# Moving the maxima products around the value products in a two-layer attention and GLU kernel

## The chip, the cores and the metric

The kernel runs on one core of one Trainium2 chip. The metric is device time in microseconds (us) of one execution; the kernel before was timed three times. Besides these times there is one profiled execution, from whose trace all rows below come.

## The reference

Four residual layers on x (2048 tokens, 448 features, float32): attention, gated unit, attention, gated unit, each on a layer-normalised input and with the same weights in both rounds. Attention has 16 heads of width 28 that share one key and one value head.

```python
q = (x @ wq).reshape(B, S, H, Dh).transpose(0, 2, 1, 3)
k = x @ wk
v = x @ wv
scores = einsum("bhqd,bkd->bhqk", q, k) * (Dh ** -0.5)
p = softmax(scores, axis=-1)
o = einsum("bhqk,bkd->bhqd", p, v)
attn = o.transpose(0, 2, 1, 3).reshape(B, S, H * Dh) @ wo

h = sigmoid(x @ w_gate) * (x @ w_up)
glu = h @ w_down

x = x + attn(layernorm(x)); x = x + glu(layernorm(x))   # twice
```

## The kernel before, in words

Tokens are cut into 16 **units** of 128 queries and keys into 16 **key tiles** of 128, so one attention layer has 16 x 16 = 256 **steps**, one for each unit and key tile; two layers have 512. Numbers that need more than half precision are carried as two float16 parts.

One step needs these products on TensorE (the profile's PE):

- four **scores** products `s` (L566): keys against queries, 96 rows deep, 128 x 512 results, four heads each. ScalarE (ACT) turns each into `P` by an exponential (L570), which frees the PSUM bank of `s`.
- one **values** step `pv` (L580 or L584): P against the values. It consists of four products side by side, each with 32 output columns. Most steps keep P in float32 (L584, two instructions to each product in the trace); at key tiles 0, 4, 8 and 12 of well-filled steps GpSimd (POOL) splits P into two float16 parts first (L603, L604), and L580 multiplies these.
- two halves of **maxima** products `mx` (L509). Softmax subtracts the row maximum, and the kernel finds it one unit ahead: it multiplies once more, 32 rows deep, and VectorE (DVE) reduces each 128 x 512 result to its maximum (L512), which frees its PSUM bank. One call of the generator `mx_gen` gives two such products, which stand in different row groups of the array; `group` calls it twice, which gives four products, one in each row group.
- **filler**: projections and the gated unit of earlier tokens (`gp`, `up`, `qp`, `kv` at L369, `dn` at L789, `wo` at L697), full 128 x 128 products that a `Filler` hands out in slices, so many ns of estimated work to a slice.

All of these but `pv` draw their PSUM results from one pool of seven banks, `psf` (L51, L98, L505 to L506, L565). The eighth bank holds the running sum of `pv`. A new tile takes a bank whose last tile has been read, and where that reading is still under way, the product waits for the engine that reads.

```python
ps = {h: psf.tile([128, 512], F32, tag=BANKS["m"], name="mx", bufs=NBK[BANKS["m"]])
      for h in (hh, hh + 1)}
for h in ps:
    nc.tensor.matmul(ps[h][:, :nk], qh[32 * h:32 * h + 32, g], KK[l][32 * h:32 * h + 32, 1, ks],
                     start=True, stop=True, tile_position=(32 * h, 0))
for h in ps:
    nc.vector.tensor_reduce(mp[:, g, h, kb:kb + 1], ps[h][:, :nk], axis=AX.X, op=OP.max)
```

The order of the work is fixed when the program is built (the kernel schedules by hand): every engine runs its instructions in the order in which the Python code emits them. In the loop over steps (L1174 to L1220) a string of letters sets that order, one pass through the string for two steps. The program calls such a pass an order; the texts below say **pass**.

- `F`: a slice of filler. Before it gives products it also emits what was put off: evaluations of finished filler results on DVE and ACT.
- `S`: one scores product and its exponential, and conversions of P that are due.
- `M`: `group`, four maxima products and their four reductions. `m`: one call of the generator, two products and two reductions.
- `P`: one values step, from a queue of finished steps.
- `T`: `finish`, which transposes the maxima of a finished unit (`mt`, L549, 16 output columns), copies them on DVE (L551) and sends them into the queries' tile `QS`.
- `X`: end of a step: deals with side work (normalisation, output projection of finished units), sets the new filler rate.

```python
order = FULL if rate > LEANR else LEAN
```

`rate` is the filler left per step in ns, and `LEANR` is 600. So passes with much filler use the string `FULL`, and passes with little, at the beginning of either layer, use `LEAN`.

In the built program the maxima products stand in groups of four 396 times and in pairs 220 times before the change; four pairs make one LEAN pass, so there are 55 of these. The scores, values, maxima and filler products are the same in number after the change as before.

Of the kernel before, what the change touches and what calls it, by code (L numbers as in the profile page):

```python
# [19 lines left out]
def interleaved_layers_kernel(ctx: ExitStack, tc: tile.TileContext, x, wq, wk, wv, wo, wg, wu, wd, out, layers=2):  # L20
# [577 lines left out]
    def convert():  # L598
        while conv:
            P, g = conv.pop(0)  # L600
            p, e = P[g], CA[g]
            h = wk1.tile([128, 2, 512], F16, name="PH", bufs=PX)
            {"A": nc.scalar.copy, "V": nc.vector.tensor_copy, "P": nc.gpsimd.tensor_copy}[e](h[:, 0], p)  # L603
            nc.gpsimd.tensor_tensor(h[:, 1], p, h[:, 0], op=OP.subtract)  # L604
            P[g] = h
# [534 lines left out]
    for b, g in sorted(qnew):  # L1140
        fill.add(qrest(b, g), QCH)

    FULL = "FSFSFSFSTPPXMFSFSFSFSFXM"
    LEAN = "FSFSmFSFSPTXmFSFSmFSFSPTXm"
    PLAG = 1
    PARTS = [False]

# [6 lines left out]
    for l in range(layers):  # L1154
# [19 lines left out]
        while step < U * KT:  # L1174
            order = FULL if rate > LEANR else LEAN
            for o in order:
                u, kt = divmod(step, KT)
                if o == "S":
                    su, skt = divmod(sn // 4, KT)
                    if sn < 4 * U * KT:  # L1180
                        scores(l, su, skt, sn % 4, P)
                        convert()
                        if order is FULL and skt in KS and l * U * KT + step >= FROM and (sn % 4 == 0 or PARTS[0]):
                            PARTS[0] = sn % 4 < 3
# [76 lines left out]
```

## Time and profile before

| what | us |
|---|---|
| median of three runs | 2257.43 |
| the three runs | 2257.43, 2257.6, 2254.36 |
| the profiled execution, its own time | 2257.6 |
| span of its trace | 2255.8 |
| PE busy | 2202.9 |
| DVE busy | 1673.9 |
| ACT busy | 1397.3 |
| POOL busy | 1045.8 |

The profiled execution is one of the three runs. Its span goes from the first to the last instruction; 1.8 us lie around it. The granted TensorE clock averages 0.997 of full speed. PE rows are pipelined and their ends are modelled, so the start of one row and the start of the next tell how long a product holds the array; the busy time alone does not.

### The profile page before, as it was taken

What the parts mean: (1) busy time and instruction counts of PE and PEld (TensorE: products, weight loads), DVE (VectorE), ACT (ScalarE), POOL (GpSimd) and SP (SyncE); (2) the same over time, 40 slices, a digit from 0 to 9 for tenths busy, and PEclk for the clock granted to TensorE, in tenths of its full rate; (3) what the DMA queues carried; (4) which work ended last, traced back from release to release, by engine and by line L of the source; (5) the groups of instructions that cost most, each with busy time, mean ns of one, the idle gap of its engine ahead of it and who ended that gap; (6) DMA issues with size and microseconds to landing.
All of it is one profiled execution on the core that took longest, in us unless ns stands there. A gap on an engine that the chain in (4) does not pass through costs nothing. (4 is left out here: it accounts for less than half of the span.)

```text
span 2255.8 us, 43048 instructions
## 1 busy us (share of the span) xinstructions
PE 2202.9 (98%) x16336; PEld 1049.5 (47%) x16336; DVE 1673.9 (74%) x2921; ACT 1397.3 (62%) x2567; POOL 1045.8 (46%) x1363
## 2 busy tenths in 40 slices
PE   8999999999999999999999999999999999999999
PEld 6322244544545444454573224545454544445457
DVE  7898887878778887774458887878787877878322
ACT  4677766666666666666425676666666666666641
POOL 4378451555445554546402014545545455454540
PEclk9999999999999999999999999999999999999999
DMA  6734542323313232332341113223232313232233
GB/s 154 212 105 133 184 158 61 93 77 103 112 52 106 67 90 80 98 96 79 102 145 57 31 47 103 85 85 101 60 94 63 102 59 102 80 95 89 78 99 123
DMA packets 224400, 217.53 MB, mean 96 GB/s; under 512 B 154048, under 2 KB 185536, under 8 KB 224192
## 3 DMA queue, kind: packets, MB, share of 16 engines
q1 hardware_dynamic: 217200, 198.89, 30.0%
q0 software_dynamic: 3680, 12.09, 1.4%
q10 hardware_dynamic: 3312, 3.79, 0.5%
q8 instruction: 128, 2.10, 0.4%
q14 instruction: 80, 0.66, 0.1%
HBM read 175.37 MB, written 23.59 MB: 88 GB/s over the span
## 5 line engine op out<-in xcount | busy, mean ns | idle before, releaser
L570 ACT ACTIVATE P<-s 128x512 f32<-128x512 f32 x2048 | 1141.3, 599 | 565.0 <-PE s L566 544.7
L512 DVE TENSOR_REDUCE mp<-mx 128x1 f32<-128x512 f32 x2048 | 1266.7, 681 | 300.6 <-PE mx L509 295.4
L566 PE MATMUL s<-QS,KK 96*128 96x512 f16 x2048 | 740.3, 381 | 21.8 <-DVE mp L512 9.2
L369 PEld LDWEIGHTS <-wgu 128*128 128x128 f16 x4928 | 459.5, 97 | 254.1 <-issue 91.6
L604 POOL TENSOR_TENSOR PH<-P,PH 128x512 f16<-128x512 f32 x384 | 458.7, 1195 | 30.8
L603 POOL CAST PH<-P 128x512 f16<-128x512 f32 x384 | 248.5, 647 | 471.5 <-ACT P L570 471.5
L584 PE MATMUL pv<-P,VV 128*32 128x512 f32 x3328 | 418.5, 599 | 0.0
L369 PE MATMUL gp<-XT,wgu 128*128 128x256 f16 x2464 | 386.1, 272 | 0.8 <-DVE mp L512 0.7
L369 PE MATMUL up<-XT,wgu 128*128 128x256 f16 x2464 | 385.3, 272 | 1.1 <-ACT P L570 0.4
L789 PE MATMUL dn<-WD,h 128*128 128x448 f16 x1344 | 330.4, 353 | 0.0
L509 PE MATMUL mx<-KK,QH 32*128 32x512 f16 x2048 | 257.2, 384 | 5.1 <-ACT P L570 3.1
L566 PEld LDWEIGHTS <-KK 96*128 96x128 f16 x2048 | 188.4, 97 | 136.0 <-issue 62.3
L509 PEld LDWEIGHTS <-QH 32*128 32x128 f16 x2048 | 62.2, 91 | 344.8 <-issue 343.3
L789 PEld LDWEIGHTS <-h 128*128 128x128 f16 x1344 | 124.7, 98 | 138.6 <-issue 23.7
L584 PEld LDWEIGHTS pv<-P,VV 128*32 128x32 f32 x3328 | 86.4, 109 | 167.5 <-issue 146.3
L764 DVE SCALAR_TENSOR_TENSOR h<-th,h 128x512 f16<-128x512 f32 x112 | 99.5, 888 | 48.4 <-ACT h L763 48.4
L763 ACT ACTIVATE h<-th 128x512 f16<-128x512 f32 x112 | 70.3, 628 | 88.0 <-DVE th L760 86.9
L760 DVE SCALAR_TENSOR_TENSOR th<-th,up 128x512 f32<-128x512 f32 x112 | 76.0, 679 | 57.2 <-PE up L369 51.7
L675 POOL TENSOR_TENSOR lb<-pvs,lb 128x512 f32<-128x512 f32 x32 | 40.7, 1270 | 138.3 <-DMA lb<-sums 119.7
L752 ACT ACTIVATE th<-gp,gsc 128x512 f32<-128x512 f32 x112 | 76.8, 686 | 42.3 <-PE gp L369 41.8
L369 PE MATMUL qp<-XT,WQ 128*128 128x512 f16 x352 | 98.4, 386 | 0.7 <-DVE ktl L412 0.7
L329 POOL TENSOR_SCALAR rs<-mv 128x1 f32<-128x1 f32 x48 | 11.0, 229 | 178.6 <-DVE mv L324 178.6
(164 smaller groups left out, 1102.9 us busy)
## 6 DMA issues: line engine op xcount, KB each, us to landing
wgu<-wgu_d SPq DMA_DIRECT2D x224, 512.0 KB
QS<-qd SPq DMA_DIRECT2D x384, 32.0 KB
lb<-sums SPq DMA_DIRECT2D x120, 64.0 KB
wgu_d<-sgu POOLq DMA_DIRECT2D x14, 512.0 KB, 3.8
qd<-qst POOLq DMA_DIRECT2D x16, 256.0 KB, 2.7
xr<-in_A_x_dram SPq DMA_DIRECT2D x16, 224.0 KB
QH<-qd SPq DMA_DIRECT2D x28, 128.0 KB
x2d<-x SPq DMA_DIRECT2D x16, 224.0 KB
```

The costliest lines, as they stand in the source:

```text
L369: nc.tensor.matmul(ps, a, b, start=n == 0, stop=n == 10)
L509: nc.tensor.matmul(ps[h][:, :nk], qh[32 * h:32 * h + 32, g], KK[l][32 * h:32 * h + 32, 1, ks], start=True, stop=True, tile_position=(32 * ...
L512: nc.vector.tensor_reduce(mp[:, g, h, kb:kb + 1], ps[h][:, :nk], axis=AX.X, op=OP.max)
L566: nc.tensor.matmul(s, KK[l][0:96, 0, kt * 128:(kt + 1) * 128], QS[l, u][:, g].rearrange("p h n -> p (h n)"), start=True, stop=True)
L570: nc.scalar.activation(p, s, AF.Exp, scale=ESC)
L584: nc.tensor.matmul(v[32 * g:32 * g + 32], VV[l][:, kt], P[g], start=kt == 0, stop=kt == KT - 1, tile_position=(0, 32 * g))
L603: {"A": nc.scalar.copy, "V": nc.vector.tensor_copy, "P": nc.gpsimd.tensor_copy}[e](h[:, 0], p)
L604: nc.gpsimd.tensor_tensor(h[:, 1], p, h[:, 0], op=OP.subtract)
L752: defer(lambda: nc.scalar.activation(th, gp.rearrange("p j n -> p (j n)"), AF.Tanh, scale=gsc))
L760: nc.vector.scalar_tensor_tensor(t, th, 1.0, up.rearrange("p j n -> p (j n)"), op0=OP.add, op1=OP.mult)
L764: defer(lambda: nc.vector.scalar_tensor_tensor(h[:, 1], t, 2.0 ** -17, h[:, 0], op0=OP.mult, op1=OP.subtract), 1)
L789: nc.tensor.matmul(p, hs[f // 2][:, a, o:o + 128], WD[:, f, c], start=n == 0, stop=n == 3 * FC - 1)
```

## The change

Two strings change, and nothing else:

```diff
-    FULL = "FSFSFSFSTPPXMFSFSFSFSFXM"
-    LEAN = "FSFSmFSFSPTXmFSFSmFSFSPTXm"
+    FULL = "FSFSFSFSTMPPXMFSFSFSFSFX"
+    LEAN = "FSFSFSFSmPTXmFSFSFSFSmPTXm"
```

In FULL, the `M` that stood at the end of a pass, after the last filler slice, now stands in front of the two values steps `PP`; the other `M` stays behind them. So eight maxima products, which were two groups of four with four scores and filler between them on either side, now stand close together, with only the values steps between, and the eight scores follow each other with filler alone between. In LEAN, the `m` that stood between the second and the third score now stands behind the fourth, in front of `P`.

On PE, a FULL pass in the built program before. The rows are in program order; `[waits X_49]` names the engine whose reading of the bank (or whose data) the row waits for; LDWEIGHTS loads the weights of the product behind it.

```order
L566 MATMUL s<-QS,KK 128x512 [waits DVE_49]
L584 MATMUL pv<-P,VV 32x512 x8
L509 LDWEIGHTS QH
L509 MATMUL mx<-KK,QH 128x512 [waits Activation_49]
L509 LDWEIGHTS QH
L509 MATMUL mx<-KK,QH 128x512 [waits DVE_49]
L509 LDWEIGHTS QH [waits PE_49]
L509 MATMUL mx<-KK,QH 128x512 [waits Activation_49]
L509 LDWEIGHTS QH
L509 MATMUL mx<-KK,QH 128x512 [waits DVE_49]
L369 LDWEIGHTS wgu
L369 MATMUL up<-XT_9966,wgu 128x256
```

The same place on PE after the change:

```order
L566 MATMUL s<-QS,KK 128x512 [waits Activation_49]
L509 LDWEIGHTS QH
L509 MATMUL mx<-KK,QH 128x512 [waits Activation_49]
L509 LDWEIGHTS QH
L509 MATMUL mx<-KK,QH 128x512 [waits Activation_49]
L509 LDWEIGHTS QH
L509 MATMUL mx<-KK,QH 128x512 [waits Activation_49]
L509 LDWEIGHTS QH [waits PE_49]
L509 MATMUL mx<-KK,QH 128x512 [waits Activation_49]
L584 MATMUL pv<-P,VV 32x512 x8
L509 LDWEIGHTS QH
L509 MATMUL mx<-KK,QH 128x512 [waits Activation_49]
```

The group of four now stands right behind the last score, and all four of its products wait for exponentials; a second group follows the values. Over the whole program, 971 maxima products waited for ACT and 1060 for DVE before, 1210 and 824 now; of the scores, 996 waited for ACT and 1032 for DVE before, 788 and 1238 now.

On PE, part of a LEAN step in the second layer before:

```order
L566 MATMUL s<-QS,KK 128x512 [waits DVE_49]
L509 LDWEIGHTS QH
L509 MATMUL mx<-KK,QH 128x512 [waits Activation_49]
L509 LDWEIGHTS QH
L509 MATMUL mx<-KK,QH 128x512 [waits DVE_49]
L566 LDWEIGHTS KK
L566 MATMUL s<-QS,KK 128x512 [waits DVE_49]
L566 LDWEIGHTS KK
L566 MATMUL s<-QS,KK 128x512 [waits Activation_49]
L584 MATMUL pv<-P,VV 32x512 x4
L509 LDWEIGHTS QH
L509 MATMUL mx<-KK,QH 128x512 [waits Activation_49]
```

The same after the change:

```order
L566 MATMUL s<-QS,KK 128x512 [waits Activation_49]
L566 LDWEIGHTS KK
L566 MATMUL s<-QS,KK 128x512 [waits DVE_49]
L509 LDWEIGHTS QH
L509 MATMUL mx<-KK,QH 128x512 [waits DVE_49]
L509 LDWEIGHTS QH
L509 MATMUL mx<-KK,QH 128x512 [waits Activation_49]
L584 MATMUL pv<-P,VV 32x512 x4
L509 LDWEIGHTS QH
L509 MATMUL mx<-KK,QH 128x512 [waits DVE_49]
L509 LDWEIGHTS QH
L509 MATMUL mx<-KK,QH 128x512 [waits Activation_49]
```

The pair that parted the four scores now stands between them and the values.

On DVE, in FULL passes of the first layer before (`th` and `h` are filler work of the gated unit, `rc` a reciprocal):

```order
L512 TENSOR_REDUCE mp<-mx 128x1 x4
L658 RECIPROCAL rc<-rc 128x16
L512 TENSOR_REDUCE mp<-mx 128x1 x4
L760 SCALAR_TENSOR_TENSOR th<-th,up 128x512
L512 TENSOR_REDUCE mp<-mx 128x1 x4
L764 SCALAR_TENSOR_TENSOR h<-th,h 128x512
```

And after, in the same part of the program:

```order
L512 TENSOR_REDUCE mp<-mx 128x1 x8
L658 RECIPROCAL rc<-rc 128x16
L760 SCALAR_TENSOR_TENSOR th<-th,up 128x512
L512 TENSOR_REDUCE mp<-mx 128x1 x8
L764 SCALAR_TENSOR_TENSOR h<-th,h 128x512
```

The reductions of the maxima now stand eight in a row, with the other work of DVE between the eights.

## The prediction

> **What bounds the kernel now.** I read the page's head first, then the busy time by stages, then who waits for whom on PE, then two stretches of the timeline.
>
> ```profile
> span 2255.8 us, 43048 instructions
> PE 2202.9 (98%) x16336; PEld 1049.5 (47%) x16336; DVE 1673.9 (74%) x2921; ACT 1397.3 (62%) x2567; POOL 1045.8 (46%) x1363
> ...
> 100.00:300.00 200.00, 187.17 (x1104) 52.66 (x1105) 173.79 (x314) 150.22 (x290) 120.80 (x106) 0.99 0.48 148
> 300.00:1050.00 750.00, 737.45 (x5639) 357.56 (x5632) 586.94 (x1004) 484.09 (x876) 382.98 (x521) 1.00 0.29 87
> 1200.00:1350.00 150.00, 146.32 (x855) 38.17 (x852) 131.27 (x225) 101.77 (x191) 16.40 (x29) 1.00 0.15 43
> 1350.00:2110.00 760.00, 756.75 (x5807) 366.27 (x5810) 599.83 (x999) 496.97 (x893) 396.26 (x496) 1.00 0.28 83
> ...
> PE s L566 <- DVE mp L512: 9.2, 28, 0.6
> PE s L566 <- ACT P L570: 5.6, 25, 0.3
> PE mx L509 <- ACT P L570: 3.1, 8, 1.1
> ```
>
> The stage rows give, after the stretch and its length, the busy time of PE, PEld, DVE, ACT and POOL. Two stages with few weight loads (100 to 300 and 1200 to 1350 us) run LEAN; the two long ones, 1510 us together, run FULL. PE is busy nearly throughout, and its waits for PSUM banks come to some 18 us in all: PE bounds the kernel. DVE stands at 78 to 79% in the FULL stages (586.94 of 750, 599.83 of 760) and at 87 to 88% in LEAN. So what PE no longer does is gained, as long as banks come free in time; that second condition is where the change can lose.
>
> The timeline of one FULL pass shows both sides. Columns: start, duration, engine, line, operation, tiles, shapes, count.
>
> ```profile
> 601.06 0.38 PE L566 MATMUL s<-QS,KK 96*128 96x512 f16 x1
> ...
> 601.28 0.38 PE L369 MATMUL gp<-XT,wgu 128*128 128x256 f16 x2
> ...
> 602.60 0.60 PE L369 MATMUL up<-XT,wgu 128*128 128x256 f16 x4
> ...
> 603.13 0.40 PE L509 MATMUL mx<-KK,QH 32*128 32x512 f16 x4
> ...
> 603.46 0.72 PE L369 MATMUL up<-XT,wgu 128*128 128x256 f16 x5
> 603.55 2.48 DVE L512 TENSOR_REDUCE mp<-mx 128x1 f32<-128x512 f32 x4 [0.36 <-PE mx L509]
> ...
> 605.98 0.38 PE L566 MATMUL s<-QS,KK 96*128 96x512 f16 x1
> ...
> 606.29 1.92 PE L584 MATMUL pv<-P,VV 128*32 128x512 f32 x16
> ...
> 608.15 0.39 PE L509 MATMUL mx<-KK,QH 32*128 32x512 f16 x4
> ...
> 608.48 0.61 PE L369 MATMUL gp<-XT,wgu 128*128 128x256 f16 x4
> ...
> 608.92 0.38 PE L566 MATMUL s<-QS,KK 96*128 96x512 f16 x1
> ...
> 609.34 0.60 ACT L570 ACTIVATE P<-s 128x512 f32<-128x512 f32 x1 [1.77 <-PE s L566]
> ...
> 609.69 0.38 PE L566 MATMUL s<-QS,KK 96*128 96x512 f16 x1
> ...
> 610.35 0.38 PE L566 MATMUL s<-QS,KK 96*128 96x512 f16 x1
> ...
> 611.75 0.40 PE L509 MATMUL mx<-KK,QH 32*128 32x512 f16 x4
> ```
>
> Starts are what counts. A score holds the array for 601.28 - 601.06 = 0.22 us where filler follows, but 606.29 - 605.98 = 0.31 where the values follow: 0.09 more. Filler of 256 columns takes 0.11 each (half of 0.22), so the four from 602.60 would let the maxima start at 603.04; they start at 603.13: 0.09 more. A group of maxima, four side by side, holds the array for 603.46 - 603.13 = 0.33 before filler, 0.11 over a single product of that width. So each change between whole-array products, products of 32 rows (`mx`) and products of 32 columns (`pv`) costs 0.09 to 0.11 us. I take 0.10.
>
> **The change, part by part.** First, fewer of these changes. A FULL pass had five (into the values, into the maxima, out; into the second maxima, out) and has four; a LEAN step had five and has four, so a LEAN pass saves two. Going through the built programs row by row and counting each place where the kind changes (the 16-column transposes count with the values) gives 1571 before and 1309 now, 262 fewer. At 0.10 that is **-26 us**.
>
> One new kind of place isn't in this trace: maxima directly in front of the values, 284 times. The nearest rows are score to values (0.09), values to maxima (two values steps hold 608.15 - 606.29 = 1.86 us) and maxima to filler (0.11). I take 0.10, as for the others. The bounds are 0, if one change serves both kinds (28 us better), and 0.31, a change and a further product's 0.22, if the values' weights can't be brought in behind maxima (57 us worse).
>
> [...]
>
> Second, the banks in a FULL pass. Seven banks go round; one belongs to the filler chain in work, so a product mostly takes the bank of the sixth tile back, and that of the fifth where two filler tiles are alive (`up` waiting for DVE while the next `gp` runs). Readiness by the rows: a score's exponential ends 609.34 + 0.60 - 608.92 = 1.02 us after the score starts; the four reductions behind 603.13 end at 2.90 (603.55 + 2.48), 0.62 apart, so the first at 1.04.
>
> - *The group behind the scores.* It now starts 0.32 after the last score (0.22 and a change), without the filler slice that stood between. Scores are 0.66 apart (609.69 to 610.35). The fourth maxima product reuses the bank of the third score from the end, 1.64 earlier (spare: 0.62), or with five banks of the second, 0.98 earlier, where 1.02 is needed. Where the filler's slice is empty, scores come 0.22 apart, exponentials only each 0.6, and the wait reaches 0.6.
> - *The scores behind the second group.* With the first group at 0, the values take 0.42 to 2.28 and the second group starts at 2.38. The eight reductions run through without a pause: 1.04, 1.66, 2.28, 2.90, then 3.52 to 5.38. The next scores come at 3.15 (0.33, then a filler slice of 0.44) and then each 0.66. The first takes the third maxima's bank (2.28, spare 0.87) or with five banks the fourth's (2.90, spare 0.25); the second 3.81 against 2.90 or 3.52; and so on for six scores. Before, only two scores in a row met such a bank, behind four reductions.
>
> These spares hold against an otherwise idle DVE. It isn't:
>
> ```profile
> L512 DVE TENSOR_REDUCE mp<-mx 128x1 f32<-128x512 f32 x680 | 421.1, 681 | 113.9 <-PE mx L509 112.9
> L764 DVE SCALAR_TENSOR_TENSOR h<-th,h 128x512 f16<-128x512 f32 x39 | 36.5, 937 | 8.4 <-ACT h L763 8.4
> L760 DVE SCALAR_TENSOR_TENSOR th<-th,up 128x512 f32<-128x512 f32 x39 | 26.5, 679 | 1.6 <-PE up L369 0.9 <-PE gp L369 0.8
> ```
>
> This is DVE from 300 to 1000 us. A pass takes 611.75 - 603.13 = 8.62 us; 8 x 0.62 = 4.96 of that is reductions, and at 78% DVE has 6.7 busy, so 1.8 us of other work, two or three pieces of about 0.68. One such piece ahead of or within the eight reductions leaves 0.19 of the larger spare and makes 0.43 of waiting out of the smaller; two make 0.49 and 1.1. Queued behind it on DVE are the rest of the eight reductions; PE waits, and nothing else runs on PE meanwhile. I take a third of the passes to go round five banks with 0.4 us of waiting, and two thirds six banks with 0.17: **0.25 us for a pass**. The bounds are 0, where every spare holds, and 0.62, one reduction late in every pass. FULL passes: 1510 / 8.62 = 175. So +44 us (0 to +109).
>
> Third, LEAN. The timeline of one step in the first layer:
>
> ```profile
> 163.15 0.60 PE L566 MATMUL s<-QS,KK 96*128 96x512 f16 x2
> 163.57 2.06 ACT L570 ACTIVATE P<-s 128x512 f32<-128x512 f32 x4 [0.77 <-PE s L566]
> ...
> 163.69 0.39 PE L509 MATMUL mx<-KK,QH 32*128 32x512 f16 x2
> ...
> 164.01 0.60 PE L566 MATMUL s<-QS,KK 96*128 96x512 f16 x2
> ...
> 164.54 1.06 PE L584 MATMUL pv<-P,VV 128*32 128x512 f32 x8
> ...
> 165.54 0.09 PEld L509 LDWEIGHTS <-QH 32*128 32x128 f16 x2 [0.84 <-issue]
> 165.54 0.39 PE L509 MATMUL mx<-KK,QH 32*128 32x512 f16 x2
> ...
> 165.86 0.61 PE L566 MATMUL s<-QS,KK 96*128 96x512 f16 x2
> 165.96 2.48 DVE L512 TENSOR_REDUCE mp<-mx 128x1 f32<-128x512 f32 x4 [0.23 <-PE mx L509]
> ```
>
> A step is 165.86 - 163.15 = 2.71 us, all of it PE's own work. Two pairs of reductions need 2.48 of these and four exponentials about 2.1 to 2.4. Four scores in a row take 0.88; the pair behind them starts 0.98 after the first, whose exponential is ready at 1.02 at best: where the bank comes from it, the 0.10 saved is waited for again. The pair behind the values meets the next four scores and then the next pair: from pair to pair lie 0.33 + 0.88 + 0.10 = 1.31 us, and its reductions need 1.66, so where the pair's banks come round this soon 0.35 is missing. I take a wait of 0.17 a step, between 0 and 0.45; 55 passes of two steps make **+19 us** (0 to +50).
>
> Nothing else on the path moves: the transposes of the maxima keep their place ahead of the next unit's scores, the values still take a step finished one earlier, and the filler slices keep their sizes, so SP's and POOL's queues see the same requests in the same order.
>
> The sum is made against the profiled execution, 2257.6 us, which lies 0.2 above the median of the runs: 2257.6 - 26 + 44 + 19 = **2295 us** (1.6% slower).
>
> **The rivals.** *The spares hold.* PE loses its 262 changes and waits as before. Place: the group directly behind the scores and the six scores behind the eight reductions. It decides at the spares above: if six banks are the rule and DVE's other pieces fall outside the eight, no score comes early. For it speaks that DVE's other work now lies between the eights in the program, and that bank waits are only 18 us now; against it that these 18 us arise at spares of 1 us and more. Time: 2257.6 - 26 = 2232, with 10 us of new waits 2242. [...]
>
> *It evens out.* New waits of 22 to 31 us meet the saving: 2253 to 2262. Nothing points to it but that it lies between.
>
> *The values' weights can't be loaded behind maxima.* Then 284 places cost 0.31 in place of 0.10, 57 us on top: 2295 + 57 = 2352, or 2232 + 57 = 2289 where the spares hold. Against it speaks that the values' weights come in beside running products behind scores.
>
> **How the numbers follow.** A difference of 0.2%, 4.5 us, is about what a measurement of this kernel can tell from none. Spares hold: 0.20. Evens out: 0.07. New waits over the saving, my forecast, with the dear values loads inside it at 0.06: 0.73. So faster 0.20, same 0.07, slower 0.73. The range runs from 2240, which takes in the dearer half of the first rival, to 2335: FULL waits of 0.45 us a pass, 35 us over the sum, and some of the bound on LEAN. Below lie some 0.1, above 0.08. The forecast's own range is 2264 to 2335.
>
> **What would show it.** In the profile after: the start from score to maxima 0.32 apart and from maxima to values also 0.32, which confirms the saving; waits of `mx` L509 for ACT P and of `s` L566 for DVE `mp` grown from 18 us to 60 or more in the list of waits, mostly at the fourth maxima product and the first scores behind the second group; PE's busy time down by about 26 us while the span grows. It is wrong if these waits stay under 26 us, or if the span grows with no wait in that list, which would put the cost into the step from maxima to values.

## The result, and the profile after

After the change the kernel takes 2288.26 us (median of four runs, 2284.79 to 2295.2), before 2256.22 (2254.36 to 2257.6): a ratio of 1.0144 with a 95% interval of 1.0131 to 1.0157. It is 1.4% slower; the forecast was 1.6% slower, 2295 us. The profiled execution took 2288.13 us, against 2257.6 before.

The page's head after the change, with the span and each engine's busy time:

```profile
span 2286.0 us, 43270 instructions
PE 2224.8 (97%) x16336; PEld 1075.9 (47%) x16336; DVE 1657.8 (73%) x2921; ACT 1376.0 (60%) x2567; POOL 1033.8 (45%) x1363
```

The busy time by stages, after the change, in the same stretches as before (PE, PEld, DVE, ACT, POOL):

```profile
100.00:300.00 200.00, 186.32 (x1108) 57.53 (x1110) 177.46 (x319) 148.15 (x290) 120.42 (x107) 0.99 0.47 148
300.00:1050.00 750.00, 735.31 (x5571) 361.01 (x5567) 572.88 (x995) 465.42 (x862) 373.01 (x515) 1.00 0.29 85
1200.00:1350.00 150.00, 146.94 (x883) 43.60 (x881) 133.62 (x229) 98.17 (x190) 19.47 (x32) 1.00 0.18 50
1350.00:2110.00 760.00, 748.46 (x5663) 365.60 (x5662) 577.64 (x975) 477.45 (x868) 374.85 (x478) 1.00 0.28 83
```

The counts say more than the busy times. In the two FULL stages PE gets 5571 and 5663 products done where it was 5639 and 5807, at nearly the same busy share; in the two LEAN stages 1108 and 883 where it was 1104 and 855. So FULL has become slower and LEAN has not. The granted clock (the first number behind POOL) is 1.00 in the FULL stages of both traces, so it isn't the clock. The starts of the same scores product (L566) in both traces put numbers on it:

| scores product | where | before | after | later by |
|---|---|---|---|---|
| 0 | first of layer 1 | 105.0 | 105.8 | 0.9 |
| 220 | LEAN is over | 283.6 | 283.9 | 0.3 |
| 1023 | last of layer 1 | 1096.6 | 1107.2 | 10.6 |
| 1024 | first of layer 2 | 1211.0 | 1222.4 | 11.4 |
| 1216 | LEAN is over | 1363.4 | 1372.6 | 9.1 |
| 2047 | last of layer 2 | 2166.6 | 2196.9 | 30.3 |

(The differences are rounded from the unrounded starts.) FULL loses 10.6 - 0.3 and 30.3 - 9.1, together **31.5 us**. LEAN gains 0.6 and 2.3, **2.9 us**. The rest, 1.7, lies at the start and between the layers.

The list of waits after the change, PE only (total, times, longest), looks as if little had happened:

```profile
PE s L566 <- DVE mp L512: 14.3, 51, 1.3
...
PE mx L509 <- ACT P L570: 3.0, 7, 1.4
PE s L566 <- ACT P L570: 3.0, 9, 0.5
...
PE mx L509 <- DVE mp L512: 2.3, 8, 0.7
```

That is 22.6 us in all where it was some 18: a rise of 4 or 5 us, where FULL alone lost 31.5. The groups of equal instructions show where to look instead. Busy time, mean of one, and idle time ahead of the maxima products, first before, then after:

```profile
L509 PE MATMUL mx<-KK,QH 32*128 32x512 f16 x2032 | 255.5, 385 | 5.0 <-ACT P L570 3.1 <-DVE mp L512 0.8
```

```profile
L509 PE MATMUL mx<-KK,QH 32*128 32x512 f16 x2032 | 294.8, 384 | 16.0 <-ACT P L570 3.0 <-DVE mp L512 2.3 <-ACT th L752 0.8
```

The same 2032 products of 0.384 us each cover 39.3 us more. Four of them that start together cover 0.40 us; four that start one after the other cover up to four times 0.38. So most of the waiting is counted as busy time of PE: in a whole group the products start 0.003 us apart (the median step in both traces) with rows of 0.384, so while one product of a group waits for its bank, the row of the product ahead of it still covers up to 0.38 us of the wait. The starts don't hide it. Within groups of maxima, the steps from one product's start to the next, counted over the whole trace, come to 22.3 us before and 74.6 after: 52 us more. Steps of 0.4 to 0.7 us there were 15 before and are 90 after.

A pass without such a wait, after the change:

```profile
610.99 0.38 PE L566 MATMUL s<-QS,KK 96*128 96x512 f16 x1
...
611.31 0.40 PE L509 MATMUL mx<-KK,QH 32*128 32x512 f16 x4
...
611.63 1.92 PE L584 MATMUL pv<-P,VV 128*32 128x512 f32 x16
611.73 4.88 DVE L512 TENSOR_REDUCE mp<-mx 128x1 f32<-128x512 f32 x8 [0.54 <-PE mx L509]
...
613.49 0.39 PE L509 MATMUL mx<-KK,QH 32*128 32x512 f16 x4
...
613.82 0.61 PE L369 MATMUL gp<-XT,wgu 128*128 128x256 f16 x4
```

Score to maxima 0.32, maxima to values 0.32, values 1.86, maxima to filler 0.33: these steps are those of the prediction. And a pass with the wait, in the second layer (timeline; PEld rows are weight loads and show when each late product went):

```profile
1914.22 4.87 DVE L512 TENSOR_REDUCE mp<-mx 128x1 f32<-128x512 f32 x8 [2.33 <-PE mx L509]
...
1918.56 0.38 PE L566 MATMUL s<-QS,KK 96*128 96x512 f16 x1
...
1919.01 0.67 DVE L760 SCALAR_TENSOR_TENSOR th<-th,up 128x512 f32<-128x512 f32 x1
...
1919.72 0.63 ACT L763 ACTIVATE h<-th 128x512 f16<-128x512 f32 x1 [0.64 <-DVE th L760]
...
1920.26 0.58 ACT L570 ACTIVATE P<-s 128x512 f32<-128x512 f32 x1
...
1920.73 0.61 ACT L681 CAST oT<-lb 128x512 f16<-128x512 f32 x1
...
1921.07 0.38 PE L566 MATMUL s<-QS,KK 96*128 96x512 f16 x1
1921.24 1.57 ACT L570 ACTIVATE P<-s 128x512 f32<-128x512 f32 x3
...
1921.38 1.70 PE L509 MATMUL mx<-KK,QH 32*128 32x512 f16 x4
1921.89 0.09 PEld L509 LDWEIGHTS <-QH 32*128 32x128 f16 x1 [0.42 <-issue]
...
1921.98 2.47 DVE L512 TENSOR_REDUCE mp<-mx 128x1 f32<-128x512 f32 x4
1922.38 0.09 PEld L509 LDWEIGHTS <-QH 32*128 32x128 f16 x1 [0.40 <-issue]
...
1923.02 1.92 PE L584 MATMUL pv<-P,VV 128*32 128x512 f32 x16
```

Read it from the top. The eight reductions hold DVE until 1919.09, so the evaluation `th` of the gated unit starts only at 1919.01. ACT's next piece `h` (L763) needs it and waits 0.64 us, and behind `h` in ACT's queue stand the exponentials: that of the score at 1918.56 starts at 1920.26, 1.70 us after it. A cast (L681) follows, and then three exponentials from 1921.24 to 1922.81. The group of maxima starts at 1921.38 and needs banks that these free. The weight loads show its second and third product going at 1921.89 and 1922.38, each 0.05 us behind the end of an exponential (1921.84 and 1922.33). The fourth starts at 1922.72 by its own row in the trace; it waits for DVE, whose first reduction of this late group ends at 1921.98 + 0.68 = 1922.66. The values start 1.64 us after the group instead of 0.32.

The same lateness stood in the kernel before, at the same place of the program:

```profile
1894.01 0.68 DVE L760 SCALAR_TENSOR_TENSOR th<-th,up 128x512 f32<-128x512 f32 x1
...
1894.72 0.63 ACT L763 ACTIVATE h<-th 128x512 f16<-128x512 f32 x1 [0.59 <-DVE th L760]
...
1896.24 1.57 ACT L570 ACTIVATE P<-s 128x512 f32<-128x512 f32 x3
...
1897.63 1.92 PE L584 MATMUL pv<-P,VV 128*32 128x512 f32 x16
...
1899.49 0.40 PE L509 MATMUL mx<-KK,QH 32*128 32x512 f16 x4
```

ACT waits 0.59 for `th`, and three exponentials run late, from 1896.24 to 1897.81. But behind the scores stood the two values steps, which draw no bank from the pool. In their 1.86 us ACT caught up, and the group of maxima at 1899.49 is whole, 0.40 us. The change puts the group in front of the values and so takes this time away.

Counted over both FULL stages of the trace after, 153 maxima products start late within their groups (14 second, 39 third and 100 fourth products; 24, all fourth, before), and the groups hold the array 49.0 us beyond their 0.33, against 7.7 before. About 36 us of it end with an exponential (116 products), 5 with ACT's other piece `th` (L752), which reads the filler's `gp` (17 products), and 8 with a reduction on DVE. The 133 products that ACT releases start 0.05 us after the end of its piece.

The exponentials are late in two ways. Of the 116 products, 65 (16.5 us) wait for one that ended less than 1.5 us after its score, and in none of these cases did another piece run on ACT between score and exponential: the maxima follow the scores too closely, or the exponentials queue behind each other. The other 51 (19.6 us) wait for one that ended 1.5 to 3 us after its score, and in 47 of these `h` stood between.

### The profile page after: what moved, and what is told of

It is laid out like the page before. It is cut to its first block, busy times and chain, and to the rows that moved or that the text cites. A ratio compares the mean times of both kernels' runs of the same rounds, so it can differ in the third digit from the quotient of the medians.

```text
span 2286.0 us, 43270 instructions
## 1 busy us (share of the span) xinstructions
PE 2224.8 (97%) x16336; PEld 1075.9 (47%) x16336; DVE 1657.8 (73%) x2921; ACT 1376.0 (60%) x2567; POOL 1033.8 (45%) x1363
## 5 line engine op out<-in xcount | busy, mean ns | idle before, releaser
L570 ACT ACTIVATE P<-s 128x512 f32<-128x512 f32 x2048 | 1126.8, 601 | 599.2 <-PE s L566 587.0
L566 PE MATMUL s<-QS,KK 96*128 96x512 f16 x2048 | 727.6, 380 | 21.2 <-DVE mp L512 14.3
L369 PEld LDWEIGHTS <-wgu 128*128 128x128 f16 x4928 | 468.2, 97 | 237.1 <-issue 69.3
L604 POOL TENSOR_TENSOR PH<-P,PH 128x512 f16<-128x512 f32 x384 | 448.4, 1168 | 30.8
L603 POOL CAST PH<-P 128x512 f16<-128x512 f32 x384 | 241.2, 628 | 480.4 <-ACT P L570 480.3
L369 PE MATMUL gp<-XT,wgu 128*128 128x256 f16 x2464 | 376.5, 272 | 0.9 <-DVE mp L512 0.9
L369 PE MATMUL up<-XT,wgu 128*128 128x256 f16 x2464 | 376.1, 272 | 0.3
L789 PE MATMUL dn<-WD,h 128*128 128x448 f16 x1344 | 323.3, 352 | 0.0
L509 PE MATMUL mx<-KK,QH 32*128 32x512 f16 x2048 | 296.6, 383 | 16.1 <-ACT P L570 3.0
L566 PEld LDWEIGHTS <-KK 96*128 96x128 f16 x2048 | 192.1, 97 | 128.3 <-issue 36.7
L764 DVE SCALAR_TENSOR_TENSOR h<-th,h 128x512 f16<-128x512 f32 x112 | 94.5, 844 | 68.5 <-ACT h L763 68.5
L763 ACT ACTIVATE h<-th 128x512 f16<-128x512 f32 x112 | 70.3, 627 | 72.2 <-DVE th L760 71.9
L752 ACT ACTIVATE th<-gp,gsc 128x512 f32<-128x512 f32 x112 | 77.1, 688 | 41.8 <-PE gp L369 41.8
```

The lines of the kernel that those rows point to most:

```text
L369: nc.tensor.matmul(ps, a, b, start=n == 0, stop=n == 10)
L566: nc.tensor.matmul(s, KK[l][0:96, 0, kt * 128:(kt + 1) * 128], QS[l, u][:, g].rearrange("p h n -> p (h n)"), start=True, stop=True)
L570: nc.scalar.activation(p, s, AF.Exp, scale=ESC)
L752: defer(lambda: nc.scalar.activation(th, gp.rearrange("p j n -> p (j n)"), AF.Tanh, scale=gsc))
L764: defer(lambda: nc.vector.scalar_tensor_tensor(h[:, 1], t, 2.0 ** -17, h[:, 0], op0=OP.mult, op1=OP.subtract), 1)
L789: nc.tensor.matmul(p, hs[f // 2][:, a, o:o + 128], WD[:, f, c], start=n == 0, stop=n == 3 * FC - 1)
```

## The experiments

The "late groups" below are this count for each kernel: time that groups of four hold the array beyond 0.33 us in the two FULL stages, 7.7 us before and 49.0 after. Diffs are against the changed kernel, unless another is named.

**Only FULL changed, only LEAN changed.** The first keeps LEAN's old string:

```diff
-    LEAN = "FSFSFSFSmPTXmFSFSFSFSmPTXm"
+    LEAN = "FSFSmFSFSPTXmFSFSmFSFSPTXm"
```

> Only the string FULL is the new one, LEAN is as before; 166 kind changes fewer by the built program, 17 us at 0.10. By the prediction's sum: -17 + 44 = +27 us, so about 2283. By the theory drawn from the changed kernel's trace (the group of maxima directly behind the scores waits for exponentials, all in FULL): the whole loss and a little more, +31 us, about 2287. If the loss lay in LEAN: 2240.

It took 2293.65 us against 2258.15 before, a ratio of 1.0156 (1.014 to 1.0172), 35.5 us slower: the whole loss is FULL's. The second keeps FULL's old string:

```diff
-    FULL = "FSFSFSFSTMPPXMFSFSFSFSFX"
+    FULL = "FSFSFSFSTPPXMFSFSFSFSFXM"
```

> Only the string LEAN is the new one; 96 kind changes fewer, 10 us. By the prediction's sum: -10 + 19 = +9 us, about 2265. By the changed kernel's trace, where the LEAN stages ended 0 to 2 us earlier: new waits eat the saving, -2 us, about 2254. If no new wait arose in LEAN: 2246.

2254.42 against 2258.15, 0.9986 (0.9976 to 0.9996): a gain of about 4 (0.9 to 5.4 by the interval). Of the 262 saved kind changes (places where whole-array, 32-row and 32-column products follow one another) LEAN has 96 by the built program and FULL 166. At 0.10 LEAN's are worth 10 us, so its new waits are some 6, not the 19 that the sum gave them. The two runs add up: 35.5 - 3.7 = 31.8, and the whole change costs 32.0.

**A slice of filler moved up to the group.** If the missing slice is the cause, putting one back between the last score and the group should help.

```diff
-    FULL = "FSFSFSFSTMPPXMFSFSFSFSFX"
+    FULL = "FSFSFSSFTMPPXMFSFSFSFSFX"
```

> Changed kernel, but FULL is FSFSFSSFTMPPXMFSFSFSFSFX: the last score and the filler slice behind it change places, so 0.44 us of filler stand between the last score and the first group of maxima; as many kind changes as in the changed kernel. If the first group waits for exponentials: some 30 to 40 us of the 41 us of late maxima behind scores go, about 2250 (2242 to 2262). If the loss comes from the eight reductions in a row and the scores behind them: nothing changes, 2285 to 2290.

2290.43 against 2258.15, 1.0146 (1.0129 to 1.0162): nothing gained. The late products are the same in number (14 second, 39 third, 101 fourth). The edit was a weak test: only the last score moved, while the products of the changed kernel mostly wait for the exponentials of the third-last score (53 products, 21.9 us) and the fourth-last (38, 9.9). The next one moves three scores:

```diff
-    FULL = "FSFSFSFSTMPPXMFSFSFSFSFX"
+    FULL = "FSSFSFSFTMPPXMFSFSFSFSFX"
```

> Changed kernel, but FULL is FSSFSFSFTMPPXMFSFSFSFSFX: the last three scores stand one filler slice (0.44 us) earlier before the first group of maxima, not only the last one as in the run before; kind changes as in the changed kernel. If the late maxima behind scores wait for exponentials that merely follow their scores too closely: most of the 35 us of such waits in FULL go, 2250 to 2262. If the exponentials are late because ACT or DVE is held up by the eight reductions: waits of several times 0.44 stay, 2275 to 2290.

2296.3 against 2258.48, 1.017 (1.0156 to 1.0184): no help either. Late groups still 48.9 us. In 22 passes the filler slices are empty, so there is nothing to move (14.4 us of waiting in both kernels); in the first groups of the other passes it fell only from 28.6 to some 26. The waits that end with an exponential stay (36 us without the shift, 37 with it); those for one that ended over 2 us after its score even rise, from 16.2 to 20.7 us. A score that comes earlier does not get its exponential earlier where ACT is behind. The idea that the spare of 0.62 us was merely a slice too small falls with it.

**Reductions of half the width.** DVE reads 256 of the 512 columns, so half of each maximum is left out and each reduction is shorter; PE's products are the same.

```diff
-  nc.vector.tensor_reduce(mp[:, g, h, kb:kb + 1], ps[h][:, :nk], axis=AX.X, op=OP.max)
+  nc.vector.tensor_reduce(mp[:, g, h, kb:kb + 1], ps[h][:, :nk // 2], axis=AX.X, op=OP.max)
```

> Changed kernel, but each reduction of the maxima reads only half of its product's columns, so half of the maxima is left out; a reduction then takes about 0.33 us for 0.62. If DVE's queue of eight reductions makes the loss: about 2245, most of the waits gone. If the exponentials on ACT make it: the late maxima behind scores stay, and only the few us go that wait for reductions, 2270 to 2280.

2217.79 against 2258.15, 0.9823 (0.9805 to 0.984), far below both expectations. But a DVE with less to do may help the kernel before as well; the control is the same edit on it:

> Kernel before, but each reduction reads only half of its product's columns (half of the maxima left out): the control of the run with half reductions on the changed kernel (2218). If DVE's queue makes the change's loss: 2230 to 2240, so that with short reductions the change gains most of the 26 us of kind changes. If not: 2190 to 2200, and the change loses as much as with whole reductions.

2213.58 against 2258.48, 0.9806 (0.9792 to 0.9819). The two rows of the reductions, first before with half the width, then after with it:

```profile
L512 DVE TENSOR_REDUCE mp<-mx 128x1 f32<-128x256 f32 x2032 | 728.1, 417 | 665.3 <-PE mx L509 659.2
```

```profile
L512 DVE TENSOR_REDUCE mp<-mx 128x1 f32<-128x256 f32 x2032 | 727.0, 417 | 485.7 <-PE mx L509 480.9
```

With reductions of 0.417 us in place of 0.68 (they cover 727.0 / 2032 = 0.358 us each; the 0.33 expected was an estimate), the change costs 2217.8 - 2213.6 = 4 us instead of 32. By the starts of the scores in these two traces FULL loses 12.7 us in place of 31.5, so 19 of its loss hang on how long DVE is held. The rest does not: late groups are still 34.7 us, some 30 of them released by ACT. Without the control the experiment would have been read wrongly: of the 70 us between this run and the changed kernel, 2258.5 - 2213.6 = 45 are gained on the kernel before as well and have nothing to do with the change.

**One ACT piece moved to DVE.** To see whether any relief of ACT helps, the cast of the normalised input (L806) goes to DVE.

```diff
-                v["hl"] = ln_split(v["x2"], *v["ls"], eng=nc.vector, hi=nc.scalar.copy)
+                v["hl"] = ln_split(v["x2"], *v["ls"], eng=nc.vector, hi=nc.vector.tensor_copy)
```

> Changed kernel, but the cast hl behind xn (L806) runs on DVE in place of ACT, so ACT no longer waits for xn behind the eight reductions (25.5 us of such ACT waits between 300 and 1060 us, 1.4 to 2.3 before the change). If holding up ACT behind DVE makes a good part of the first layer's loss: 2288 - 5 to 10 = about 2280. If scores simply lie too near: 2288 to 2292.

2287.92 against 2258.48, 1.0137 (1.012 to 1.0153): no difference to the changed kernel that can be measured. ACT's waits for these casts' input, 25.5 us in the first layer, are gone from this trace, and yet the late groups of that layer are as long (25.5 us, 25.7 in the changed kernel): these waits of ACT do not stand where the maxima need it.

**The two groups apart.** One group stays in front of the values, the other goes back to the end of the pass, so that reductions come four at a time again.

```diff
-    FULL = "FSFSFSFSTMPPXMFSFSFSFSFX"
+    FULL = "FSFSFSFSTMPPXFSFSFSFSFXM"
```

> Changed kernel, but FULL is FSFSFSFSTMPPXFSFSFSFSFXM: the first group stays directly behind the scores in front of the values, the second goes back to the end of the pass, so the reductions come in fours again; five kind changes a pass as before (1496 in all). If the near scores alone make the loss: about 2254 + 30 = 2284. If the eight reductions in a row make it: as the run with LEAN alone changed, plus 2 us for the kind changes of the transposes, 2254 to 2260.

2300.29 against 2258.48, 1.0186 (1.0172 to 1.02), slower still. PE's waits in this kernel:

```profile
PE mx L509 <- DVE th L760: 5.8, 19, 1.4
PE s L566 <- DVE mp L512: 5.7, 20, 0.4
PE mx L509 <- DVE mp L512: 5.2, 22, 0.7
PE mx L509 <- ACT P L570: 4.4, 7, 2.5
```

The scores no longer wait more than before (5.7), but the maxima now wait for DVE too, since only four scores, about 3.1 us, lie between the group at the end of a pass and the next. Late groups rise to 61.9 us, of which some 22 are released by ACT, none of those by an exponential that ended more than 2 us after its score. Two things follow. The group in front of the values is late through ACT even where reductions come four at a time, so its place alone costs. And the very late exponentials of the changed kernel do come from the eight in a row.

**The ACT piece behind `th` put off.** In the pass shown, ACT stands still because `h` is next in its queue and `th` is not there. The program puts `h` off by two filler slices behind `th`; six gives DVE time to finish. The piece of DVE that follows `h` (L764) moves along with it.

```diff
-                    defer(parts, 2)
+                    defer(parts, 6)
```

> Changed kernel, but the copy h on ACT (L763) is put off by six filler slices in place of two, so that it stands behind more exponentials in ACT's order and no longer holds them up while th waits behind the eight reductions on DVE. If exponentials are late because ACT is held up by th: the waits of maxima whose exponential ended over 2 us after its score (36 of them, 16 us) mostly go, 2288 - 10 to 16 = about 2275. If scores are merely too near, or DVE alone makes the waits: 2285 to 2290.

2272.15 against 2258.56, 1.0061 (1.0042 to 1.0081): 16 us less than the changed kernel, as the chain through ACT wanted. ACT's wait, first in the changed kernel, then with `h` later (total, times, longest):

```profile
ACT h L763 <- DVE th L760: 71.9, 55, 5.5
```

```profile
ACT h L763 <- DVE th L760: 33.1, 12, 7.3
```

Late products whose exponential ended 2 to 3 us after its score fall from 36 (16.2 us) to 4 (1.4 us), late groups from 49.0 to 37.2 us. Part of the lateness only shrinks: those at 1.5 to 2 us rise from 15 products (3.4 us) to 36 (10.0). Waits for DVE in late groups fall too, from 8 to 3.5 us. The control is the same edit on the kernel before:

> Kernel before with the same putting off of h: the control. Its first group of maxima stands behind the values, the second behind a filler slice, and few of its maxima are late, so under either theory 2252 to 2260.

2251.42 against 2258.56, 0.9974 (0.9959 to 0.9989), a little better than expected: the wait costs the kernel before something as well (86.9 us and 57 times there, 32.3 and 12 with the edit). By the starts of the scores, the change costs FULL 19.0 us between these two kernels and 31.5 between the original ones (by the times, 2272.15 - 2251.42 = 20.7 against 32.0): some 12 of its loss hang on where `h` and L764 stand. ACT's wait for `th` is no longer after the change than before (71.9 against 86.9); what is new is that maxima stand behind it.

**Both theories together.** If moved slices and a faster DVE only help jointly, three scores shifted and half reductions at once should win clearly (half of each maximum is left out again).

```diff
-    FULL = "FSFSFSFSTMPPXMFSFSFSFSFX"
+    FULL = "FSSFSFSFTMPPXMFSFSFSFSFX"
...
-  nc.vector.tensor_reduce(mp[:, g, h, kb:kb + 1], ps[h][:, :nk], axis=AX.X, op=OP.max)
+  nc.vector.tensor_reduce(mp[:, g, h, kb:kb + 1], ps[h][:, :nk // 2], axis=AX.X, op=OP.max)
```

> Both conditions taken away at once: FULL is FSSFSFSFTMPPXMFSFSFSFSFX, with the last three scores a filler slice earlier, and each reduction reads half of the columns (half of the maxima left out). If the loss needs both the near scores and the long queue of reductions: the saving of kind changes comes out, the 2214 of the kernel before with half reductions less 15 to 26, 2188 to 2200. If the near scores alone, by their position, make the rest: as the changed kernel with half reductions, 2215 to 2220.

2215.67 against 2258.56, 0.9809 (0.9789 to 0.983): the same as half reductions alone. Late groups remain at 31.5 us. The joint theory falls; a slice more in front of the group is worth nothing here.

**The best of the parts.** The new LEAN, the old FULL, and `h` later:

```diff
-    FULL = "FSFSFSFSTMPPXMFSFSFSFSFX"
+    FULL = "FSFSFSFSTPPXMFSFSFSFSFXM"
...
-                    defer(parts, 2)
+                    defer(parts, 6)
```

> New LEAN, old FULL, and h put off by six slices: what the runs so far point to as the best. If the putting off helps the old FULL by a little: 2248 to 2253; if it does nothing: 2254 as with the new LEAN alone; if the later h makes its products wait: 2256 and over.

2247.31 against 2258.56, 0.995 (0.9935 to 0.9964). It beats both kernels, and its 11 us are the sum of LEAN's 4 and the later `h`'s 7.

## Why the prediction was right, and where it was not

*The saved kind changes.* Right. From start to start over all such places, score to values takes 0.31 us, score to maxima 0.325, maxima to filler 0.33 to 0.34 (0.317 in the median), and the place that no trace had shown, maxima to values, 0.308 over 284 places (0.314 in the median): 0.09 above the 0.22 that a score of the same width holds the array in front of filler, between the bounds of 0 and 0.31, at the value taken. The 262 are worth 26 us, and the rival of dear values' weights is out.

*The banks in FULL.* Right in size: the forecast put +44 us of waits in FULL. Its 166 saved changes are worth 17 us, so measured are 31.5 + 17 = 48 us of new waits. Right too that the fourth product bears most of it (100 of 153), and that an empty slice costs about 0.6: in 22 passes, all late, it was 14.4 / 22 = 0.65.

*How the 48 are made up.* Here the working failed, and that the size still fits is in part luck. It weighed two places alike, and blamed DVE's other pieces within the eight reductions. The second place, the scores behind the eight, costs little: the step from filler to score grew from 0.152 to 0.156 us, 6 us over the kernel. The first, the group behind the scores, costs most of 49.0 - 7.7 = 41 (43.0 of the 49 stand at this group). And its spare was worked out with an exponential that is ready 1.02 us after its score; where ACT has lost time in its queue, it is 1.1 to 3 us. Of the 36 us that end with an exponential, only 5.0 belong to exponentials that ended less than 1.12 us after their score; 11.5 lie at 1.12 to 1.5 us, 3.4 at 1.5 to 2 and 16.2 at 2 to 3. The chain that makes the latest ones (eight reductions, `th` behind them, `h` behind `th`, exponentials behind `h`) was not in the prediction at all. It is shown by the trace and, together with the later L764, by the runs with a later `h`.

*LEAN.* The term of +19 us was mis-sized: about 6 was measured, and LEAN by itself gains 4. It was taken as a middle between 0 and 0.45 a step; the measured 0.05 (6 / 110) lies near the lower bound.

*The proof that was named.* Wrong. The prediction wanted 60 us in the list of waits, called itself refuted below 26, and expected PE's busy time to fall by 26. The list shows 22.6 and busy time rose by 2224.8 - 2202.9 = 21.9. By that test the forecast would have been dropped, although the starts show the waits: the test read busy rows and idle time between them, in spite of the prediction's own remark that starts are what counts.

*The rivals.* In FULL the spares did not hold and it did not even out. LEAN alone came out between the two: 4 us gained of the 10 saved.

*What stays open.* Of FULL's 48 us, 19 hang on the length of the reductions and some 12 on the place of `h` and L764; whether the 12 lie wholly inside the 19 wasn't separated. With the short reductions 12.7 + 17 = 30 remain, mostly as late groups that ACT releases. That ACT's ordinary queue, some tenths of a us behind at the end of four scores, makes most of these is what the counts say, but no run took that queue away. Why three shifted scores don't help is in part argued: the counts show exponentials that end as late as before, and that a slice of four products (0.44 us) is too little against exponentials that run each 0.5 to 0.6 us behind one another is an estimate from these rows. Taking `h` or the cast at L681 off ACT altogether, or an eighth bank, was not tried.

## What to carry to other kernels

Before moving work in an order written by hand, ask what the work that it passes was good for besides its own result: here the values steps, which need no bank of the pool, were the 1.86 us in which ScalarE caught up, and that was worth more than the saved kind changes. Count what one engine waits for through a third (DVE to ACT to PE), and take a spare from the late passes of the trace, not from a clean one. And where products stand side by side in the array, look for waits in the starts: here busy time hid them, and the list of waits grew by only 4 or 5 us.

## What the runs showed of the hardware

- A maxima product that waited for a bank started 0.05 us after the end of the ACT piece that freed it (133 products in the trace after the change).
- Of four maxima products in different row groups, one that comes late was not made up for: where the fourth was over 0.1 us late and values followed (72 groups in the FULL stages after the change), the values started 0.300 to 0.302 us behind it, about as long as behind the fourth product of a whole group (0.300 to 0.315, 116 groups), so that its lateness was lost in full.
- Changing from products of 32 rows straight to products of 32 columns took 0.308 us from start to start in the mean, 0.314 in the median (284 places after the change), about as much as from maxima to filler (median 0.317) or from a score to values (0.310); a score in front of filler took 0.22.
